# A Mamba-2 scan feeding a branch-train-merge FFN: the opening stage of the kernel in another order

## The chip, the cores and the metric

The kernel runs on one core of one Trainium2 chip. A core has five engines that run side by side, each with its own queue of instructions in order: TensorE (matrix products, called PE in the profile, with PEld for its weight loads), VectorE (DVE), ScalarE (ACT), GpSimd (POOL) and SyncE (SP), which here only issues DMA transfers. Engines wait for one another through semaphores. Products go to PSUM[...]; everything else works in SBUF, and the inputs, the outputs and some intermediate results lie in DRAM.

The metric is the device time of one execution in microseconds, as the median of several runs. "Chunk" is used below for 128 tokens of one sequence. "Step" is used for one half of one expert applied to one block of 512 tokens.

## The reference, cut to what matters

The first part is a Mamba-2 scan in chunks, the second a sum over four experts weighted by normalised probabilities.

```python
# x (4, 8, 768, 32), a (4, 8, 768), B and C (4, 8, 768, 16); all float32
log_a = np.log(np.clip(a, 1e-6, 1.0))
for each chunk:
    cum = np.cumsum(la, axis=-1)
    L = np.exp(cum[..., :, None] - cum[..., None, :]) * causal
    y_intra = einsum('bhij,bhjd->bhid', (C @ B^T) * L, x)
    y_inter = einsum('bhin,bhnd->bhid', C, state) * exp(cum)[..., None]
    y = y_intra + y_inter
    state = exp(sum(la)) * state + sum_j B_j x_j exp(cum[-1] - cum_j)

x = y.transpose(0, 2, 1, 3).reshape(3072, 256)        # heads side by side
p = probs / (probs.sum(-1, keepdims=True) + 1e-9)     # (3072, 4)
for e in range(4):                                    # w1 (4, 256, 1024), w2 (4, 1024, 256)
    out += p[:, e:e+1] * (maximum(x @ w1[e], 0) @ w2[e])
```

## The kernel before, in words

**Tiling.** The 3072 tokens are 24 chunks of 128. The four sequences go side by side: chunks 0 to 3 are the first chunks of the four sequences, chunks 4 to 7 their second ones, and so on, so that four chunks make a block of 512 tokens (`CPB = 4`), and there are six blocks. An FFN step takes one expert and one half of its hidden width, so a block has eight steps and the whole program 48, numbered n.

**The scan of a chunk c.** `load_tokens` (L104) brings x, B, B transposed and C transposed into `xb`. The decays a come to all 128 partitions in one of three ways, chosen by `spread` (L289) and `load_decays` (L109):

- for chunks 0 and 1 (below `SPREAD = 2`) a small tile `a_q` holds the rows, and TensorE spreads them over the partitions by a product with ones or with a mask, into the PSUM banks X and Y (chunk 0: also acc2 and acc3);
- for chunk 2 (below `DIRECT = 3`) a DMA reads the input a with a broadcast over the partitions into `ab` (512 KB written), and VectorE clips it and writes zeros in the first columns (L330, L331);
- from chunk 3 on a DMA reads the clipped copy `acut_d` in DRAM, which `store_decays` (L248) has written.

From the decays, `decay_part` (L315) makes the triangular decay matrices `LT` with two or four VectorE scans (L342), and GpSimd makes the weighted B columns of `MT` (L347). `masks` (L351, ScalarE) prepares C for two heads at a time, `scores` (L358, TensorE) makes C B^T in four PSUM banks, `masked` (L371, VectorE) multiplies scores and decays into `MT`, `outputs` (L379) multiplies `MT` by x on TensorE, and ScalarE copies the result into `yT`, the input of the FFN, and into `A`, from which `carry` (L405, VectorE) makes the state for the next chunk of the sequence.

**The FFN.** Its first products go to the banks X and Y and its second ones to the accumulators acc0 to acc3 (one PSUM bank each). Two PSUM banks with the tag `att` serve scores and outputs. Steps 0 and 1 (`PLAIN = 2`) are plain: `plain_first(n, b)` (L487) makes the first products of step n on half b of the block (256 tokens, two chunks), `gated` (L462, VectorE) does the maximum with zero and multiplies by the gate, and `plain_second` (L505) makes the second products. From step 2 on each step is a Strassen-like scheme with seven products instead of eight: `fmul`, `snap`, `total`, `diff`, `smul` (L434 to L517). It needs sums and differences of the block of inputs (`sums`, L421, four VectorE instructions) and of the weights. The latter are made on GpSimd in the first block (`sums_of`, L158) and stored to DRAM together with the weights, for the five blocks that follow.

**Gates.** The normalised probabilities are made by GpSimd, turned by TensorE and copied to `p_sb` (L264 to L266), and stored to DRAM as `p_d` by a DMA on ScalarE's queue (L267). `load_gate` (L281) reads a row from there with a broadcast to all partitions, on SP's queue. The gate of the first expert for the first block is made differently, by `spread_gate` (L269): four small products straight from `p_sb` and one ScalarE copy.

**What sets the order.** The schedule is written out by hand: each engine takes its instructions in the order in which the program's lines issue them. Lines 652 to 730 are the opening (four chunks, the two plain steps, and the first part of chunk 4). The loop at L733 then runs steps 2 to 47, with the pieces of later chunks between the products. Loads are issued on SP's queue in program order and may wait for a buffer[...].

Of the kernel before, what the change touches and what calls it, by code (L numbers as in the profile page):

```python
# [12 lines left out]
P = 128  # L13
NQ, NT = 4, 2
# [3 lines left out]
def kernel(  # L18
# [57 lines left out]
    def real(c):  # L76

        return c % CPB * NBLK + c // CPB
# [20 lines left out]


    st = {}
    SPREAD, DIRECT = 2, 3

    def load_tokens(c):  # L104
        xb = load.tile([P, W], FP32, tag="xb", name="xb", bufs=4)
        nc.sync.dma_start(out=xb, in_=xbc[real(c)])
        st.setdefault(c, {})["xb"] = xb

    def load_decays(c, queue):  # L109
        if c >= SPREAD:  # L110
            ab = load.tile([P, NH * P], FP32, tag="ab", name="ab")
            nc.sync.dma_start(
                out=ab, in_=(a if c < DIRECT else acut_d)[real(c)].rearrange(
                    "h s -> (h s)").partition_broadcast(P))
            st.setdefault(c, {})["ab"] = ab
        if c >= CPB:
            ah = st[c]["ah"] = load.tile([HN, P], FP32, tag="ah", name="ah")
            queue.dma_start(out=ah, in_=ac_d[real(c)].unsqueeze(1).to_broadcast([NH, N, P]))
# [61 lines left out]
    pr = const.tile([P, T // P, E], FP32, name="pr")  # L180
    a_sb = const.tile([NCH * NH // 2, 2, P], FP32, name="a_sb")

    a_q = const.tile([P, SPREAD, NT, P], FP32, name="a_q")
    nc.gpsimd.memset(a_q[:, 0], 0.0)
    nc.vector.memset(a_q[:, 1:], 0.0)
    nc.scalar.dma_start(out=pr, in_=probs)
# [5 lines left out]
        out=a_sb, in_=a.rearrange("c h s -> (c h) s").rearrange("(p r) s -> p r s", r=2))  # L192
    load_tokens(0)
    load_tokens(1)
    load_decays(2, nc.sync)
    load_w1(0)
    load_tokens(2)


    ident = const.tile([P, NQ, P], FP32, name="ident")  # L200
# [25 lines left out]
    def clip(engine, v, top=1.0):  # L226
        engine.tensor_scalar(out=v, in0=v, scalar1=1e-6, scalar2=top, op0=ALU.max, op1=ALU.min)
# [18 lines left out]
    nc.gpsimd.memset(a_cut[:, :, 0:1], 0.0)  # L246

    def store_decays():  # L248
        nc.sync.dma_start(
            out=acut_d.rearrange("c h s -> (c h) s").rearrange("(p r) s -> p r s", r=2), in_=a_cut)  # L250
        nc.sync.dma_start(
            out=ac_d.rearrange("c h s -> (c h) s").rearrange("(p r) s -> p r s", r=2), in_=a_sb)

    gate = {}
# [5 lines left out]
    def turn_gates():  # L260

        rows = T // P * E
        pp = ps_att.tile([rows, P], FP32, tag="att", name="pp")
        nc.tensor.transpose(pp, pr.rearrange("p i e -> p (i e)"), ident[:, 0])  # L264
        gate["rows"] = p_sb = const.tile([rows, P], FP32, name="p_sb")
        nc.scalar.copy(out=p_sb, in_=pp)  # L266
        nc.scalar.dma_start(out=p_d.rearrange("i e s -> (i e) s"), in_=p_sb)  # L267

    def spread_gate():  # L269

        p_sb = gate["rows"]
        g = ps_att.tile([P, CPB, P], FP32, tag="att", name="gp")
        for i in range(CPB):
            r = real(i) * E
            nc.tensor.matmul(
                out=g[:, i], lhsT=ident[:T // P * E, 0, r:r + 1].to_broadcast([T // P * E, P]),
                rhs=p_sb, start=(i == 0), stop=True, skip_group_check=True)
        gate[0, 0] = ffn.tile([P, CPB, P], FP32, tag="gate", name="gate", bufs=3)
        nc.scalar.copy(out=gate[0, 0], in_=g)
# [6 lines left out]

    yT, yS = {}, {}

    def spread(c):  # L289


        s = st[c]
        if c == 0:
            s["a"] = []
            for q, (pool, tag) in enumerate(((ps_f, "X"), (ps_f, "Y"), (ps_s, "acc2"), (ps_s, "acc3"))):
                k = slice(32 * q, 32 * q + 32)
                b = pool.tile([P, NT * P], FP32, tag=tag, name="a")
                nc.tensor.matmul(
                    out=b, lhsT=ones[k], rhs=a_q[k, c].rearrange("p t s -> p (t s)"),
                    start=True, stop=True, tile_position=(32 * q, 0))  # L300
                s["a"].append(b)
            return
        b = [ps_f.tile([P, 2, NT * P], FP32, tag=tag, name="a") for tag in ("X", "Y")]
        for q in range(NQ):
            nc.tensor.matmul(
                out=b[q // 2][:, q % 2], lhsT=qmask[:, q, 0:1].to_broadcast([P, P]),
                rhs=a_q[:, c].rearrange("p t s -> p (t s)"), start=(q % 2 == 0), stop=True,
                skip_group_check=True)
        s["a"] = [v.rearrange("p q s -> p (q s)") for v in b]

    def decays(c):
        for part in range(3):
# [2 lines left out]
    def decay_part(c, part):  # L315
# [10 lines left out]
            return  # L326
        half = NH * P // 2
        if part == 0:
            if SPREAD <= c < DIRECT:
                clip(nc.vector, s["ab"])  # L330
                nc.vector.memset(s["ab"].rearrange("p (h s) -> p h s", h=NH)[:, :, 0:1], 0.0)  # L331
            if c >= SPREAD:
                s["a"] = [s["ab"][:, :half], s["ab"][:, half:]]
            LT = att.tile([P, NH * P], FP32, tag="LT", name="LT", bufs=1)
            s["LT"] = LT.rearrange("p (h s) -> p h s", h=NH)

            s["MT"] = att.tile([P, NH, P + N], FP32, tag="MT", name="MT")
# [149 lines left out]
    def plain_first(n, b, a=(0, 1)):  # L487

        k = n // SPB
        cols = slice(b * HB - HB, b * HB)  # L490
        f = first.setdefault(n, {})
        for bank, ws in [(("X", (A11, A12)), ("Y", (S3, A22)))[i] for i in a]:
            f[bank] = ps_f.tile([P, JJ, HB], FP32, tag=bank, name=bank)
            for j in range(JJ):
                for i, w in enumerate(ws):
                    nc.tensor.matmul(  # L496
                        out=f[bank][:, j], lhsT=wt1[n][:, w, j * P:j * P + P],
                        rhs=yT[k][:, i, cols], start=(i == 0 and j == 0), stop=(i == 1),
                        skip_group_check=True)
# [157 lines left out]
    scores(0, homes)  # L657
    decays(0)
    spread(1)
    load_tokens(3)  # L660
    store_decays()
    load_w1(1)
    load_w2(0)
    load_decays(3, nc.sync)
    masked(0, range(NQ))
    divide_gates()
    sum_w1(0, 0)
    masks(1)
    decays(1)
    turn_gates()  # L670
    scores(1, banks)
    spread_gate()
    outputs(0, ps_att, "att")
    load_w2(1)
    load_w1(2)
    load_w2(2)
    sum_w1(1, 0)
    masked(1, range(NQ))
    outputs(1, ps_att, "att")
    masks(2)  # L680
    load_chunk(4)
    load_gate(0, 1)
    load_w1(3)
    load_w2(3)

    plain_first(0, 1, (0,))
    scores(2, banks)
    plain_first(0, 1, (1,))
    decays(2)
    sum_w2(0, 0)  # L690
    masked(2, range(NQ))
    masks(3)
    outputs(2, ps_att, "att")
    load_chunk(5)
    gated(0, "11", "X")

    scores(3, homes)
    decays(3)
    sum_w2(1, 0)
    gated(0, "21", "Y")  # L700
    plain_first(1, 1)
    masked(3, range(NQ))
    plain_gated(1, 1)
    plain_second(0, 1, 1)
    outputs(3, ps_att, "att")
    sum_w1(2)
    sum_w2(2)
    load_w1(4)
    load_w2(4)
    plain_second(0, 1, 2)  # L710
    masks(4)
    plain_first(0, 2)
# [12 lines left out]
    scores(4, ((ps_att, "att"), (ps_att, "att"), (ps_f, "X"), (ps_f, "Y")))  # L725
    masked(4, (2, 3, 0, 1))
    plain_second(1, 1, 2)
    sums(0)
    for c in range(1, CPB):
        carry(c)  # L730


    for n in range(PLAIN, NS):  # L733
# [127 lines left out]
```

## Time and profile before

| what | value |
|---|---|
| median of 5 runs | 667.01 us (665.47 to 667.9) |
| the profiled execution | 667.01 us, of which the span on the page is 665.2 us |
| TensorE busy | 648.1 us, 97% of the span, 3359 products |
| VectorE busy | 497.5 us, 75% |
| ScalarE and GpSimd busy | 115.7 us and 115.3 us, 17% each |
| DMA | 127.34 MB, mean 191 GB/s |

The page's chain follows the work that ended last back to the start, and says what share of the span each engine holds in it. In the listings by time, each row is a merged group of instructions of one line: its start and length in microseconds, the engine, the line of the kernel, what it writes and reads, how many, and in brackets how long the engine sat idle before it and what released it. A TensorE product in 32-bit numbers shows as two records, so four products of a bank show as x8. "Granted clock" is the share of TensorE's full clock in a stretch.

### The profile page before, as it was taken

To read this page: it belongs to the slowest core of one execution; us is meant where nothing else is said; L and a number is where in the kernel's file an instruction comes from. 1 tells how busy PE (TensorE), PEld (TensorE's weight loads), DVE (VectorE), ACT (ScalarE), POOL (GpSimd) and SP (SyncE) were. 2 spreads that over 40 slices of the span, in tenths; PEclk is the share of its full clock that TensorE was granted. 3 is DMA by queue.
4 is the path that set the end of the run, shared out by engine and by line. 5 is a ranking of instruction groups with operands and counts; after the bars stand their busy time and mean duration, and the time that the engine had idled before them with its cause. 6 is when DMAs were issued, how large, how long until landed. Compare 5 with 4: busy or idle time off the path is not lost.

```text
span 665.2 us, 8906 instructions
## 1 busy us (share of the span) xinstructions
PE 648.1 (97%) x3359; PEld 542.4 (82%) x3359; DVE 497.5 (75%) x813; ACT 115.7 (17%) x247; POOL 115.3 (17%) x157
## 2 busy tenths in 40 slices
PE   7999999999999999999999999999999999999997
PEld 4777878888888887888887888888788888888886
DVE  7488798787787688867878778678867776856655
ACT  3111211122112121221121112212111112111110
POOL 5776494020000002000003000000200000200000
PEclk9898999999999999999999999999999999999999
DMA  8987999414768610678640556941266862077000
GB/s 254 317 325 293 354 361 310 153 46 130 241 221 329 225 56 17 241 248 293 246 160 1 191 181 232 361 182 56 76 238 192 299 212 76 17 243 240 6 1 32
DMA packets 68274, 127.34 MB, mean 191 GB/s; under 512 B 26616, under 2 KB 50056, under 8 KB 68232
## 3 DMA queue, kind: packets, MB, share of 16 engines
q1 hardware_dynamic: 65404, 111.77, 48.9%
q0 software_dynamic: 2304, 14.68, 5.3%
q8 instruction: 26, 0.43, 0.3%
q10 hardware_dynamic: 524, 0.34, 0.2%
q14 instruction: 16, 0.13, 0.1%
HBM read 108.69 MB, written 18.07 MB: 191 GB/s over the span
## 4 chain that ended last, share of the span: by engine, by line
PE 87%; DVE 9%; issue 1%; DMA 1%; POOL 1%; ACT 0%; SPq 0%; ACTq 0%; DVEq 0%; POOLq 0%
PE acc L532 39%; PE X L448 22%; PE Y L448 18%; DVE hT L477 3%; PE g L365 2%; PE y L394 2%; DVE MT L375 1%; PE acc L513 1%; PE X L496 1%; PE Y L496 1%; DVE z L460 1%; PE y L388 1%; DVE h L470 1%; DMA wt<-in_w_dram 1%; DMA a_sb<-in_a_dram 0%
## 5 line engine op out<-in xcount | busy, mean ns | idle before, releaser
L532 PE MATMUL acc<-hT,wt 128*128 128x256 f32 x736 | 183.1, 382 | 0.0
L460 DVE TENSOR_TENSOR z<-Y,snap 128x512 f32<-128x512 f32 x138 | 94.5, 685 | 116.3 <-ACT snap L455 99.1
L455 ACT COPY snap<-X 128x512 f32<-128x512 f32 x138 | 80.9, 586 | 476.6 <-PE X L448 476.6
L532 PEld LDWEIGHTS acc<-hT,wt 128*128 128x128 f32 x736 | 138.3, 190 | 24.0 <-issue 6.0
L448 PE MATMUL X<-yS,wt 128*128 128x256 f32 x552 | 142.4, 381 | 0.0
L532 PE MATMUL acc<-h,wt 128*128 128x256 f32 x552 | 141.5, 379 | 0.0
L448 PEld LDWEIGHTS X<-yS,wt 128*128 128x128 f32 x552 | 105.5, 191 | 14.5
L532 PEld LDWEIGHTS acc<-h,wt 128*128 128x128 f32 x552 | 104.9, 190 | 14.3
L470 DVE SCALAR_TENSOR_TENSOR h<-z,gate 128x512 f32<-128x512 f32 x138 | 98.8, 716 | 3.5 <-PE acc L513 0.4
L448 PE MATMUL Y<-yT,wt 128*128 128x256 f32 x368 | 94.4, 379 | 0.0
L477 DVE TENSOR_TENSOR hT<-h,hT 128x512 f32<-128x512 f32 x92 | 76.3, 829 | 3.2
L448 PEld LDWEIGHTS Y<-yT,wt 128*128 128x128 f32 x368 | 68.8, 190 | 10.6
L477 DVE TENSOR_TENSOR hT<-h,h 128x512 f32<-128x512 f32 x92 | 63.5, 714 | 0.8
L448 PE MATMUL Y<-yS,wt 128*128 128x256 f32 x184 | 50.8, 399 | 8.9 <-DVE z L460 8.9
L342 DVE TENSOR_TENSOR_SCAN LT<-ab,ident 128x512 f32<-128x512 f32 x44 | 54.9, 1250 | 0.2 <-POOL MT L347 0.2
L347 POOL TENSOR_TENSOR MT<-xb,LT 128x128 f32<-128x128 f32 x20 | 8.7, 434 | 251.9 <-PE Y L448 133.8
L375 DVE TENSOR_TENSOR MT<-g,LT 128x256 f32<-128x256 f32 x96 | 33.9, 415 | 20.8 <-PE g L365 20.8
L448 PEld LDWEIGHTS Y<-yS,wt 128*128 128x128 f32 x184 | 33.4, 192 | 19.2 <-DVE z L460 12.7
L448 PE MATMUL X<-yT,wt 128*128 128x256 f32 x184 | 47.3, 380 | 0.0
L325 POOL TENSOR_TENSOR cts<-ctm,dec 128x256 f32<-128x256 f32 x20 | 18.5, 926 | 161.5 <-ACT snap L455 158.2
L470 DVE SCALAR_TENSOR_TENSOR h<-X,gate 128x512 f32<-128x512 f32 x50 | 34.3, 686 | 10.0 <-PE X L496 5.3
L448 PEld LDWEIGHTS X<-yT,wt 128*128 128x128 f32 x184 | 34.9, 190 | 5.1 <-DVE MT L375 0.3
(96 smaller groups left out, 341.8 us busy)
## 6 DMA issues: line engine op xcount, KB each, us to landing
wt<-w_d SPq DMA_DIRECT2D x80, 896.0 KB, 10.3
w_d<-wt POOLq DMA_DIRECT2D x16, 896.0 KB, 7.1
ab<-acut_d SPq DMA_DIRECT2D x21, 512.0 KB, 5.3
wt<-in_w_dram SPq DMA_DIRECT2D x32, 256.0 KB, 7.1
xb<-in_xbc_dram SPq DMA_DIRECT2D x24, 320.0 KB, 4.7
gate<-p_d SPq DMA_DIRECT2D x23, 256.0 KB, 9.5
out_dram<-ot SPq DMA_DIRECT2D x160, 16.0 KB, 5.3
ah<-ac_d SPq DMA_DIRECT2D x20, 64.0 KB
```

What stands on the lines that cost most here:

```text
L325: nc.gpsimd.tensor_mul(cts, s["ctm"], dec.unsqueeze(1).to_broadcast([HN, NT, P]))
L342: nc.vector.tensor_tensor_scan(out=LT[:, i * w:i * w + w], data0=s["a"][i], data1=ident.rearrange("p h s -> p (h s)")[:, :w], initial=0.0, ...
L365: nc.tensor.matmul(out=g.rearrange("p t s -> p (t s)"), lhsT=s["xb"][k, OBT:OBT + P], rhs=s["ctm"][k].rearrange("p t s -> p (t s)"), start ...
L375: nc.vector.tensor_mul(s["MT"][:, h, 0:P], s["g"][q], s["LT"][:, h])
L394: nc.tensor.matmul(out=y[32 * q:32 * q + 32, t, 0:w], lhsT=xb[:, h * D:h * D + D], rhs=MT[:, NT * q + t, 0:w], start=(first and t == 0), s ...
L448: nc.tensor.matmul(out=f[bank][:, j], lhsT=wt1[n][:, w, j * P:j * P + P], rhs=rhs, start=(i in (1, 2, 5) and j == 0), stop=(j == JJ - 1), ...
L455: nc.scalar.copy(out=s, in_=first[n]["X"])
L460: nc.vector.tensor_add(z, first[n]["Y"], first[n][i])
L470: nc.vector.scalar_tensor_tensor(out=h, in0=first[n][src], scalar=0.0, in1=g.unsqueeze(1).to_broadcast([P, JJ, HB]), op0=ALU.max, op1=ALU. ...
L477: nc.vector.tensor_sub(h[o], h[x], h[y])
L496: nc.tensor.matmul(out=f[bank][:, j], lhsT=wt1[n][:, w, j * P:j * P + P], rhs=yT[k][:, i, cols], start=(i == 0 and j == 0), stop=(i == 1), ...
L532: nc.tensor.matmul(out=acc[k, u][:, half], lhsT=w2_op(n, w)[:, j], rhs=rhs[:, j], start=(begins and j == 0), stop=(n % SPB == SPB - 1 and ...
```

## The change

Five things change, all in the opening stage and in what follows from it:

- **Third chunk's decays.** `SPREAD` goes from 2 to 3 and `DIRECT` is gone: chunk 2 takes its decays through `a_q` and TensorE, as chunk 1 does, in two halves (bank X, bank Y) that can be issued apart. The broadcast load of a for chunk 2 and VectorE's clip of it are gone. `a_q` has room for three chunks and lies in the buffer that the tile `o` uses later.
- **Loads.** On SP's queue the four `xb` loads of chunks 0 to 3 and the weights of steps 0 and 1 (`w1`) and of step 0 (`w2`) are issued at the start, with chunks 0 to 2 ahead of the first weights. The stores of `store_decays` move from SP's queue to ScalarE's.
- **Banks.** The first products of step 0 on half 1 go to acc2 and acc3 instead of X and Y.
- **Gates.** `spread_gate` is gone; the first gate is fetched from `p_d` by `load_gate(0, 0)` on SP's queue.
- **Order.** GpSimd's first weight sums come after the decays of chunk 2, the scores of chunk 2 come before the first FFN products, the gated products of step 0 come after the decays of chunk 3, `sums(0)` comes before the second half of the plain stage instead of after it, and of the carries of chunks 1 to 3 only the first stays there; those of chunks 2 and 3 go to the ends of steps 3 and 4.

```diff
-    SPREAD, DIRECT = 2, 3
+    SPREAD = 3
@@ load_decays
-                out=ab, in_=(a if c < DIRECT else acut_d)[real(c)].rearrange(
+                out=ab, in_=acut_d[real(c)].rearrange(
@@
-    a_q = const.tile([P, SPREAD, NT, P], FP32, name="a_q")
+    a_q = ffn.tile([P, SPREAD, NT, P], FP32, tag="o", name="a_q", bufs=1)
@@
     load_tokens(0)
     load_tokens(1)
-    load_decays(2, nc.sync)
+    load_tokens(2)
     load_w1(0)
-    load_tokens(2)
+    load_tokens(3)
+    load_w1(1)
+    load_w2(0)
@@ store_decays
-        nc.sync.dma_start(
+        nc.scalar.dma_start(
...
-        nc.sync.dma_start(
+        nc.scalar.dma_start(
@@
-    def spread_gate():
...
-    def spread(c):
+    def spread(c, halves=(0, 1)):
...
-        b = [ps_f.tile([P, 2, NT * P], FP32, tag=tag, name="a") for tag in ("X", "Y")]
-        for q in range(NQ):
-            nc.tensor.matmul(
-                out=b[q // 2][:, q % 2], lhsT=qmask[:, q, 0:1].to_broadcast([P, P]),
...
+        for i in halves:
+            b = ps_f.tile([P, 2, NT * P], FP32, tag="XY"[i], name="a")
+            for q in range(2):
+                nc.tensor.matmul(
+                    out=b[:, q], lhsT=qmask[:, 2 * i + q, 0:1].to_broadcast([P, P]),
...
@@ decay_part
-            if SPREAD <= c < DIRECT:
-                clip(nc.vector, s["ab"])
-                nc.vector.memset(s["ab"].rearrange("p (h s) -> p h s", h=NH)[:, :, 0:1], 0.0)
@@ plain_first
-            f[bank] = ps_f.tile([P, JJ, HB], FP32, tag=bank, name=bank)
+            pool, tag = (ps_f, bank) if n or b > 1 else (ps_s, {"X": "acc2", "Y": "acc3"}[bank])
+            f[bank] = pool.tile([P, JJ, HB], FP32, tag=tag, name=bank)
@@ the opening
     spread(1)
-    load_tokens(3)
-    store_decays()
-    load_w1(1)
-    load_w2(0)
-    load_decays(3, nc.sync)
     masked(0, range(NQ))
     divide_gates()
-    sum_w1(0, 0)
     masks(1)
+    store_decays()
     decays(1)
     turn_gates()
     scores(1, banks)
-    spread_gate()
+    masks(2)
+    spread(2, (0,))
     outputs(0, ps_att, "att")
+    spread(2, (1,))
+    sum_w1(0, 0)
+    masked(1, range(NQ))
+    outputs(1, ps_att, "att")
+    load_decays(3, nc.sync)
     load_w2(1)
     load_w1(2)
     load_w2(2)
+    scores(2, homes)
+    plain_first(0, 1)
+    decays(2)
     sum_w1(1, 0)
-    masked(1, range(NQ))
-    outputs(1, ps_att, "att")
-    masks(2)
+    masks(3)
+    load_gate(0, 0)
     load_chunk(4)
     load_gate(0, 1)
     load_w1(3)
     load_w2(3)
-    plain_first(0, 1, (0,))
-    scores(2, banks)
-    plain_first(0, 1, (1,))
-    decays(2)
-    sum_w2(0, 0)
     masked(2, range(NQ))
-    masks(3)
     outputs(2, ps_att, "att")
-    load_chunk(5)
-    gated(0, "11", "X")
     scores(3, homes)
     decays(3)
-    sum_w2(1, 0)
-    gated(0, "21", "Y")
+    load_chunk(5)
+    load_w1(4)
+    load_w2(4)
+    sum_w2(0, 0)
+    plain_gated(0, 1)
     plain_first(1, 1)
     masked(3, range(NQ))
+    sum_w2(1, 0)
     plain_gated(1, 1)
+    outputs(3, ps_att, "att")
     plain_second(0, 1, 1)
-    outputs(3, ps_att, "att")
     sum_w1(2)
     sum_w2(2)
-    load_w1(4)
-    load_w2(4)
+    sums(0)
     plain_second(0, 1, 2)
...
     plain_second(1, 1, 2)
-    sums(0)
-    for c in range(1, CPB):
-        carry(c)
+    carry(1)
@@ the loop over steps
+        if PLAIN < n <= CPB:
+            carry(n - 1)
         if c_out is not None:
             carry(c_out)
```

More of the change, by code (lines that the diff above doesn't have):

```diff
@@ L264, in turn_gates @@
         nc.tensor.transpose(pp, pr.rearrange("p i e -> p (i e)"), ident[:, 0])
-        gate["rows"] = p_sb = const.tile([rows, P], FP32, name="p_sb")
+        p_sb = const.tile([rows, P], FP32, name="p_sb")
         nc.scalar.copy(out=p_sb, in_=pp)
         nc.scalar.dma_start(out=p_d.rearrange("i e s -> (i e) s"), in_=p_sb)
-    def spread_gate():
[L271 to L274, printed above, removed]
-            nc.tensor.matmul(
[L276 to L279, printed above, removed]
     def load_gate(k, e):
@@ L302, in spread @@
             return
-        b = [ps_f.tile([P, 2, NT * P], FP32, tag=tag, name="a") for tag in ("X", "Y")]
-        for q in range(NQ):
-            nc.tensor.matmul(
-                out=b[q // 2][:, q % 2], lhsT=qmask[:, q, 0:1].to_broadcast([P, P]),
-                rhs=a_q[:, c].rearrange("p t s -> p (t s)"), start=(q % 2 == 0), stop=True,
-                skip_group_check=True)
-        s["a"] = [v.rearrange("p q s -> p (q s)") for v in b]
+        for i in halves:
[3 more added lines that the diff above has]
+                    out=b[:, q], lhsT=qmask[:, 2 * i + q, 0:1].to_broadcast([P, P]),
+                    rhs=a_q[:, c].rearrange("p t s -> p (t s)"), start=(q == 0), stop=True,
+                    skip_group_check=True)
+            s.setdefault("a", []).append(b.rearrange("p q s -> p (q s)"))
     def decays(c):
```

## The prediction

> **What bounds the kernel now.** I read the page's chain first, then TensorE by time, then what its gaps wait for on VectorE and ScalarE, then the clock by stretches, then the DMA landings. The chain:
>
> ```profile
> PE 87%; DVE 9%; issue 1%; DMA 1%; POOL 1%; ACT 0%; SPq 0%; ACTq 0%; DVEq 0%; POOLq 0%
> ```
>
> TensorE sets the end; only its holes can be won. From 70 us on, the holes are at most 1.5 us each, and the instruction lists of the two programs as built agree there but for two carries. So the case is the first 70 us. I write (n, b) for the first products of step n on block half b, and c in brackets for a chunk: y(3), masked(3). TensorE by time (start, length, idle before and releaser in brackets):
>
> ```profile
> 14.98 0.70 PE L394 MATMUL y<-MT,xb 128*32 128x144 f32 x16 [1.93 <-POOL MT L347]
> 16.16 3.44 PE L496 MATMUL X<-yT,wt 128*128 128x256 f32 x8 [0.48 <-ACT yT L400]
> 20.36 1.99 PE L496 MATMUL Y<-yT,wt 128*128 128x256 f32 x8
> ...
> 50.66 2.07 PE L448 MATMUL Y<-yS,wt 128*128 128x256 f32 x4 [1.89 <-DVE z L460]
> 52.52 1.81 PE L448 MATMUL X<-yS,wt 128*128 128x256 f32 x4
> 68.18 1.13 PE L448 MATMUL Y<-yS,wt 128*128 128x256 f32 x4 [0.72 <-DVE z L460]
> ```
>
> Twice a hole is followed by matmuls of double length: 3.44 us against 1.99 for the same shape at 20.36. The clock by stretches (busy and count of PE, PEld, DVE, ACT, POOL; granted clock; DMA):
>
> ```profile
> 13.14:16.55 3.41, 1.08 (x18) 0.80 (x19) 3.17 (x5) 1.76 (x7) 2.85 (x4) 1.00 0.94 260
> 16.55:19.97 3.42, 3.42 (x12) 2.33 (x14) 0.51 (x1) 0.81 (x3) 3.26 (x5) 0.50 1.01 316
> 47.27:50.69 3.42, 1.53 (x22) 0.85 (x20) 3.32 (x7) 1.05 (x3) 2.78 (x5) 1.00 0.78 317
> 50.69:54.10 3.41, 3.41 (x8) 2.78 (x9) 3.00 (x2) 0.00 (x0) 3.23 (x4) 0.50 1.03 418
> 149.68:153.09 3.41, 2.04 (x9) 1.82 (x10) 3.16 (x6) 0.47 (x3) 0.95 (x2) 1.00 0.00 0
> ```
>
> A stretch busy for 1.08 or 1.53 of 3.41 us is followed by one at half clock, about 1.7 us lost each; one busy for 2.04 is not. The second hole comes from VectorE, where the sums of the block and three carries stand ahead of z:
>
> ```profile
> 42.88 1.40 DVE L426 TENSOR_TENSOR yS<-yT 128x256 f32<-128x256 f32 x1
> 44.31 0.83 DVE L427 TENSOR_TENSOR yS<-yT,yS 128x256 f32<-128x256 f32 x1
> ...
> 49.93 0.68 DVE L460 TENSOR_TENSOR z<-Y,snap 128x512 f32<-128x512 f32 x1
> ```
>
> ScalarE by time shows the gates' store p_d holding the queue, although p_sb was ready at 10.99:
>
> ```profile
> 10.73 0.26 ACT L266 COPY p_sb<-pp 96x128 f32<-96x128 f32 x1 [3.01 <-PE pp L264]
> 13.93 0.33 ACTq L267 DMA_DIRECT2D p_d<-p_sb  x1
> 14.30 0.59 ACT L279 COPY gate<-gp 128x512 f32<-128x512 f32 x1 [3.30 <-DMA wt<-in_w_dram]
> ```
>
> And the transfers of p_d (the store and two fetches of gates, to 60 us):
>
> ```profile
> DMA to landing us min/median/max: 6.3/6.5/10.6
> ```
>
> [...] L426 takes 1.40 us here, 0.42 at 129.83 with GpSimd idle.
>
> **The change, part by part.**
>
> *Start.* The VectorE memset of a_q doubles to 128x512: 128x128 takes 0.17, 128x256 0.27, so 0.48, 0.2 us later for all that follows. The third chunk's two clips and memset (2 x 0.28 + 0.06) lie in VectorE's 0.87 us wait before the first scan; without that cover they cost 0.6. VectorE drops the clip and memset of ab (0.68 + 0.07), off the path. Four spreads of 128x256 (four warm such products: 1.73 us) replace gp's four of 128x128 (1.16), in the idle time at 13 to 15; exposed they would cost 0.6.
>
> *GpSimd.* MT of chunk 1 no longer stands behind the first weight sums (L160 to L162, 2.3 us), so the 1.93 us hole goes. What is late next is ScalarE. acut_d and ac_d move to its queue after the second mask (7.72); the list of the changed program makes ac_d wait for xb of chunk 2 (about 8.2) and p_d wait for ac_d's landing. ac_d took 5.3 us: 8.4 + 5.3 = 13.7. Behind p_d stand masks(2) (0.69), yT and A of chunk 0 (0.57) and of chunk 1 (0.56), so X of product (0,1) starts near 16.3, as before. Bounds: 15.4 if the stores overtake the loads (then y of chunk 1 and its copies bind), 17.2 if ac_d takes 6.3. I take 16.3. scores(2), 0.83 us between X and Y before, are now done in that wait. In the window 13.14 to 16.55 TensorE has half a spread and y(1) until 14.5 (1.36), scores (0.5) and the start of X (0.25): about 2.1 of 3.41, near the 2.04 that kept its clock. So no half clock.
>
> *SP's queue.* It loses ab of chunk 2 (512 KB) and the two stores (issue 0.34 and 0.54), so the weights move up: w1(0), landed at 10.98 before, by about 10; w1(1), 14.55 before, by about 13. Both are there before their products: nothing. ab(3) waits on SP for acut_d's landing, which moves from 12.86 to about 13.5, with six weight loads queued behind it; its scan comes after masked(2), near 17.5, and it had landed at 19.39, so VectorE may wait a microsecond for it. That lies under the wait for the gate below. a_q in the buffer of o costs nothing, since o is first written at step 8.
>
> *Other banks.* acc2 and acc3 for (0,1) leave X and Y to (1,1), which can run before the gates come: (0,1), y(2), scores(3) with its 0.6 us wait for A, and (1,1) end at 16.3 + 3.46 + 0.63 + 1.27 + 3.46 + 0.2 = 25.3.
>
> *Gates by DRAM.* gate(0,0) came from gp's copy at 14.9; now p_d is stored (13.7 + 6.3 = 20.0 at most) and fetched through SP behind w2(1), w1(2), w2(2). Bytes decide: before, 5.78 MB up to w2(2) had landed at 23.99. After, 5.52 MB up to the gate: 0.26 MB less at 360 GB/s is -0.7, start +0.2[...]. It lands at 23.8; from 22 (no loss) to 30.6 (20.0 + 10.6). On VectorE masked(3) is queued behind both products with this gate, and y(3) on TensorE behind masked(3): gated 1.34 + masked 1.40 + y 0.63 (0.3 overlapped) + two second products 3.65 gives 23.8 + 6.7 = 30.5 for the start of (0,2). It was 32.02: -1.5.
>
> *Plain stage.* sums(0), 4.0 us, move ahead of the gated product of (0,2), into idle time that VectorE had from 28.6 to 33.9; they run near 28 to 32, and X of (0,2) is ready at 32.2. Two carries leave as well. With scores(4) at 39.3, masked(4) (1.42), carry(1) (0.5 to 1.2) and the snap of X (near 43.3) before it, z of step 2 ends at about 44.0; TensorE needs it at 48.77 - 1.5 = 47.3. That gives -1.89 for the hole and -1.75 for its half clock (3.51 us for work of 1.73). With the sums still uncovered z would end at 48.0, a hole of 0.7.
>
> *Carries.* carry(2) after step 3 lies before a z ended at 79.07 for a matmul of 80.37: 1.3 of cover. carry(3) after step 4 stands before the z that TensorE waited 1.50 us for at 96.24: +0.5 (0.20 + 0.29), up to 1.6 with GpSimd beside it. I take 0.5.
>
> *Later loads.* The gate's issue (0.39) and its wait for p_d stand on SP ahead of xb(4) and ab(4), issued at 19.47 and 20.21 before; they come within a microsecond of that, and ab(4) is first scanned near 33. No later weight is late either: w1(6) is summed from 82.06 and used at 106.7. Cover of over 10 us: nothing.
>
> Sum: -1.5 - 1.89 - 1.75 + 0.5 = -4.6 against the profiled execution's 667.01 (span 665.2 and 1.8 around it), which is also the median of the runs: 662.4.
>
> **Rivals.**
>
> *Half clock stays.* The new waits, near 15 and between 25 and 26.3, meet one window with too little work: +1.7, 664.1. For it: [...] 2.1 is close to 2.04. Against: each wait is shorter than 1.89.
>
> *The gate decides.* Slower from a landing at 28.4 (23.8 + 4.6). If p_d and its fetch take the longest rows, 14.0 + 6.3 + 10.6 = 30.9, (0,2) starts at 37.6, +5.6 - 3.1: 669.5. Against: 10.6 was met behind a full queue and weight stores at 31.6.
>
> *Given back.* VectorE stays behind at the ends of steps 2 to 4 (holes 0.72, 1.50, 0.36), since GpSimd's weight sums slow it and their pace is the loads', which don't move. TensorE then waits until the time at which it used to arrive, and nothing is left: 667.0. Against: 68.18's chain starts with a TensorE product (scores at 59.45) and moves along.
>
> *Better.* The gate at 22.2 and the 0.72 hole gone: -1.6 - 0.7 more, 660.1 to 661.
>
> **How the numbers follow.** Forecast 0.50 (its own range 661.2 to 663.6), half clock 0.20, better 0.12, given back 0.09, gate decides 0.09. The time is the first case's. Low 660.0 takes in "better", high 666.5 half clock and a gate two microseconds later; about 2 in 10 is outside. A difference under 0.2% (1.3 us) can't be told from none: faster 0.82, same 0.09, slower 0.09.
>
> **What would show it.** Right: one half-clock stretch fewer after 16 us and none near 50; VectorE's L470 of (0,1) waiting for the gate's DMA until 23 to 25; y(3) on TensorE held by masked(3); no hole at step 2; the hole after step 4 at 2 us. ScalarE's p_d at about 13.7 shows the wait for ac_d, at 11.5 the overtaking. Wrong: a gate after 28, a half-clock stretch in the new waits, or holes of steps 3 to 5 grown by more than 2 us together.

## The result and the profile after

The changed kernel takes 665.0 us in the median (663.37 to 668.27, 43 runs), the kernel before 666.15 us beside it (80 runs): a ratio of 0.9989, 95% interval 0.998 to 0.9999. The forecast was 662.4 us, with a range from 660.0 to 666.5. The time lies inside that range, but the change is a gain of a tenth of a per cent, barely clear of none, where seven tenths were forecast.

The profiled execution of the changed kernel takes 664.69 us (span 662.9), 2.32 us less than that of before. Its page's chain, where TensorE still carries the end:

```profile
PE 88%; DVE 8%; DMA 2%; issue 1%; SPq 0%; ACT 0%; POOL 0%; ACTq 0%; DVEq 0%; POOLq 0%
```

TensorE by time in the changed kernel (start, length, then idle time before it and its releaser in brackets; L485 and L502 are the plain stage's first and second products, L436 the first products of later steps, L376 and L382 the outputs y):

```profile
16.10 1.99 PE L485 MATMUL X<-yT,wt 128*128 128x256 f32 x8
...
23.48 1.89 PE L485 MATMUL Y<-yT,wt 128*128 128x256 f32 x8
28.18 0.92 PE L382 MATMUL y<-MT,xb 128*32 128x144 f32 x16 [2.80 <-DVE MT L363]
...
32.58 1.89 PE L485 MATMUL X<-yT,wt 128*128 128x256 f32 x8
...
49.25 1.13 PE L436 MATMUL Y<-yS,wt 128*128 128x256 f32 x4
...
91.31 0.70 PE L376 MATMUL y<-cts,M 128*128 128x256 f32 x2 [0.59 <-POOL cts L316]
...
93.87 1.13 PE L436 MATMUL Y<-yS,wt 128*128 128x256 f32 x4 [1.24 <-DVE z L448]
```

Three of the forecast's marks are there: X of (0,1) starts at 16.10 and runs at full length, nothing waits at step 2 (49.25, no bracket), and no stretch before the tail runs at half clock (the granted clock is 1.00 from 16.55 to 655 us, and 0.999 in the mean of the execution). One wait is longer than forecast: TensorE stands for 2.80 us before y(3), where the forecast's own sum leaves some 1.2 us (from 25.3 to 23.8 + 1.34 + 1.40), and (0,2) starts at 32.58 and not at 30.5. Why, VectorE by time shows:

```profile
25.75 0.69 DVE L458 SCALAR_TENSOR_TENSOR h<-X,gate 128x512 f32<-128x512 f32 x1 [5.16 <-PE Y L485]
...
26.95 1.41 DVE L363 TENSOR_TENSOR MT<-g,LT 128x256 f32<-128x256 f32 x4
```

VectorE idles for 5.16 us. The bracket names Y of (0,1), but that product had ended at 19.8, so it was another of the instruction's waits: the gate. Its way begins on ScalarE, which by time shows the store (L269):

```profile
13.66 0.31 ACTq L269 DMA_DIRECT2D p_d<-p_sb  x1
14.02 0.69 ACT L344 ACTIVATE ctm<-xb,tmask 128x128 f32<-128x128 f32 x2 [3.05 <-DMA ac_d<-a_sb]
```

It goes on in SP's queue, by time, with the fetch (L273) behind the last of the weights:

```profile
15.63 1.27 SPq L146 DMA_DIRECT2D wt<-in_w_dram  x2
18.88 0.37 SPq L273 DMA_DIRECT2D gate<-p_d  x1
```

And the landings of the gates that are fetched in the first 60 us:

```profile
DMA to landing us min/median/max: 6.3/7.4/11.9
```

The store is issued at 13.66, as forecast, and has landed by 18.88, when SP is let go (it had issued nothing since 16.90); the shortest fetch, 6.3 us, is the first one, so the gate lands at 25.2. Working down from there: (0,2) is 0.56 us later than before, not 1.5 earlier; y of chunk 5, in step 3, starts at 63.57 against 66.24 (2.67 earlier, since the hole and the half clock of step 2 are gone); y of chunk 6, in step 5, at 91.31 against 93.52 (2.21 earlier); TensorE ends at 658.79 against 661.10 (2.31 earlier).

### The profile page after: what moved, and what is told of

It is laid out like the page before. It is cut to its first block, busy times and chain, and to the rows that moved or that the text cites. A ratio compares the mean times of both kernels' runs of the same rounds, so it can differ in the third digit from the quotient of the medians.

```text
span 662.9 us, 8905 instructions
## 1 busy us (share of the span) xinstructions
PE 645.5 (97%) x3359; PEld 540.5 (82%) x3359; DVE 496.3 (75%) x814; ACT 115.1 (17%) x246; POOL 113.1 (17%) x157
## 4 chain that ended last, share of the span: by engine, by line
PE 88%; DVE 8%; DMA 2%; issue 1%; SPq 0%; ACT 0%; POOL 0%; ACTq 0%; DVEq 0%; POOLq 0%
PE acc L521 39%; PE X L436 22%; PE Y L436 18%; DVE hT L465 4%; PE g L353 2%; PE acc L502 2%; PE y L382 2%; DVE MT L363 1%; PE X L485 1%; PE Y L485 1%; PE y L376 1%; DMA xb<-in_xbc_dram 1%; DMA ac_d<-a_sb 1%; DVE z L448 1%; DVE h L458 0%
## 5 line engine op out<-in xcount | busy, mean ns | idle before, releaser
L436 PE MATMUL X<-yS,wt 128*128 128x256 f32 x552 | 141.7, 379 | 0.0
L436 PEld LDWEIGHTS X<-yS,wt 128*128 128x128 f32 x552 | 104.9, 190 | 14.3
L436 PE MATMUL Y<-yT,wt 128*128 128x256 f32 x368 | 94.4, 379 | 0.0
L436 PEld LDWEIGHTS Y<-yT,wt 128*128 128x128 f32 x368 | 68.8, 190 | 10.6
L436 PE MATMUL Y<-yS,wt 128*128 128x256 f32 x184 | 49.8, 393 | 6.8 <-DVE z L448 6.8
L436 PE MATMUL X<-yT,wt 128*128 128x256 f32 x184 | 47.2, 379 | 0.0
L436 PEld LDWEIGHTS Y<-yS,wt 128*128 128x128 f32 x184 | 32.9, 189 | 16.8 <-DVE z L448 10.3
L436 PEld LDWEIGHTS X<-yT,wt 128*128 128x128 f32 x184 | 35.0, 190 | 4.8
```

The source lines that it names most:

```text
L436: nc.tensor.matmul(out=f[bank][:, j], lhsT=wt1[n][:, w, j * P:j * P + P], rhs=rhs, start=(i in (1, 2, 5) and j == 0), stop=(j == JJ - 1), ...
```

## The experiments

Every kernel was timed in five rounds. The kernel before took 665.7 us (59 runs) beside the first four, 665.21 (25) beside the next four and 665.68 (35) beside the last four; ratios are to these.

| run | made from | median us | ratio, 95% interval |
|---|---|---|---|
| e1 | changed kernel, first gate by TensorE again | 663.75 | 0.9962 (0.9949 to 0.9974) |
| e2 | kernel before, sums early, two carries later | 665.55 | 0.9995 (0.9983 to 1.0008) |
| e3 | changed kernel, gate fetched first | 663.25 | 0.9954 (0.9933 to 0.9975) |
| e4 | e1, store of the gates later | 664.3 | 0.9966 (0.9952 to 0.9979) |
| e5 | changed kernel, cts ahead of the second weight sums | 663.86 | 0.9972 (0.9959 to 0.9985) |
| e6 | e1 and the same | 662.38 | 0.9949 (0.9933 to 0.9965) |
| e7 | e3 and the same | 661.15 | 0.9927 (0.9912 to 0.9943) |
| e8 | e2 and the same | 663.92 | 0.9973 (0.996 to 0.9985) |
| e9 | kernel before, hole of step 2 filled | 665.52 | 0.9997 (0.9982 to 1.0012) |
| e10 | kernel before, cts ahead of the second weight sums | 665.71 | 0.9998 (0.9981 to 1.0015) |
| e11 | e7, carries later | 659.16 | 0.9911 (0.9892 to 0.993) |
| e12 | kernel before, first gate by DRAM | 670.54 | 1.0085 (1.006 to 1.0109) |

The theory after comparing the two profiles: the gate's fetch cost the forecast its first term. The rival: the gate only hides that the gains are given back further on. The first four runs try both.

### e1: the first gate by TensorE again

```diff
+    def spread_gate():    # four products from p_sb into a bank att, one ScalarE copy: as before
...
     scores(1, banks)
+    spread_gate()
...
     masks(3)
-    load_gate(0, 0)
     load_chunk(4)
```

> The changed kernel with one part undone: the first gate comes from four TensorE products and a ScalarE copy again, not from DRAM. Theory (the wait for the first gate's DMA is what ate the gain): VectorE's gated product of (0,1) starts near 20.6 instead of 25.75, the 2.8 us hole before y(3) is gone, TensorE reaches (0,2) near 29.8 instead of 32.58, span 2.7 us shorter than the changed kernel's, and fewer runs with a half-clock stretch; median near 661.6. Rival (the hole only shows a lateness that the next wait takes over, in VectorE, GpSimd or the weights): (0,2) or step 2 is late all the same, and the time stays within 1 us of the changed kernel's 665.0.

Measured: 663.75 us, 0.9962. TensorE by time, around y(3) (here L394):

```profile
26.03 0.70 PE L394 MATMUL y<-MT,xb 128*32 128x144 f32 x16
...
30.21 1.89 PE L497 MATMUL X<-yT,wt 128*128 128x256 f32 x8
```

The hole before y(3) is gone and (0,2) starts at 30.21, 0.3 from the forecast's 30.5. TensorE ends at 656.73 instead of 658.79. So the late gate costs 2.06 us in the profile, just what the forecast missed in that term. The median gains less and misses the theory's 661.6 by 2 us. The granted clock says why in part: 16 of the 21 executions have a mean of 0.996 to 0.997, and the profiled one is among the five above. Executions with a like clock agree with the profile: at 0.999 or more 662.77 against the changed kernel's 664.44, at 0.996 to 0.997 664.09 against 666.36 (the two kernels were timed on different occasions).

### e2: the sums and carries of the change alone

```diff
     sum_w2(2)
     load_w1(4)
     load_w2(4)
+    sums(0)
     plain_second(0, 1, 2)
...
     plain_second(1, 1, 2)
-    sums(0)
-    for c in range(1, CPB):
-        carry(c)
+    carry(1)
...
+        if PLAIN < n <= CPB:
+            carry(n - 1)
         if c_out is not None:
             carry(c_out)
```

> The kernel before with one part of the change alone: the sums of the first block ahead of the second half of the plain stage, carries of chunks 2 and 3 at the ends of steps 3 and 4. Theory: the 1.89 us hole of step 2 goes, and with it the half-clock stretch that follows it in some runs; the hole after step 4 grows by up to 0.6. Time 1.5 to 3 us shorter than the kernel before, so this part alone gives more than the whole change's 1.2. Rival (VectorE is late at step 2 for another reason): less than 0.5 us.

Measured: 665.55 us, 0.9995: no gain, where the theory had 1.5 to 3 us. TensorE by time:

```profile
47.25 1.13 PE L448 MATMUL Y<-yS,wt 128*128 128x256 f32 x4
...
91.13 0.70 PE L388 MATMUL y<-cts,M 128*128 128x256 f32 x2 [2.09 <-POOL cts L325]
...
92.56 2.08 PE L448 MATMUL Y<-yS,wt 128*128 128x256 f32 x4
```

And GpSimd by time, the first of the weight sums and the cts that TensorE waits for:

```profile
79.70 0.80 POOL L160 TENSOR_TENSOR wt<-wt 128x256 f32<-128x256 f32 x1 [9.99 <-DMA wt<-in_w_dram]
...
90.36 0.71 POOL L325 TENSOR_TENSOR cts<-ctm,dec 128x256 f32<-128x256 f32 x1
```

The hole at step 2 is gone, as meant. But at step 5 TensorE now stands for 2.09 us before y of chunk 6, which it had reached without a wait before, and the products behind run at half clock (2.08 us for what takes 1.13; the mean granted clock of this execution is 0.997). It waits for cts, which GpSimd makes behind the weight sums of two steps (79.70 to 89.6), and these had waited 9.99 us for weights to land. TensorE came 4.4 us earlier than before (y of chunk 5 at 61.88 against 66.24), and cts only 2.1 (90.36 against 92.50): the loads had not moved as far.

### e3: the gate fetched ahead of the second weights

```diff
     load_decays(3, nc.sync)
+    load_gate(0, 0)
     load_w2(1)
...
     masks(3)
-    load_gate(0, 0)
```

> The changed kernel with the first gate's fetch issued on SP ahead of the weights w2(1), w1(2) and w2(2) instead of behind them. In the instruction list as built, the gates' store p_d then also waits for an earlier load than ac_d. Theory: the gate lands near 20 instead of 25.2, VectorE does not wait for it, TensorE reaches (0,2) near 29, span 3 to 3.5 us shorter than the changed kernel's. Rival (bytes: the weights pushed back by 3 us become the wait, at GpSimd's sums or at the second products): the time stays within 1 us of the changed kernel's.

Measured: 663.25 us, 0.9954; the span is 661.7 us, 1.2 shorter than the changed kernel's, where 3 to 3.5 were expected. (0,2) starts at 29.29, and TensorE has no wait for the gate any more. The fetch is issued at 14.32 instead of 18.88. Part of that was not aimed at: in the program as built ScalarE no longer waits for ac_d, and p_d goes out at 11.01. Step 5 takes back what it can: 2.36 us of waiting for cts before y of chunk 6, and half clock behind it (2.08 us for Y's 1.13).

### e4: the store of the gates behind the outputs of chunk 1

```diff
-        nc.scalar.dma_start(out=p_d.rearrange("i e s -> (i e) s"), in_=p_sb)
+    def store_gates():
+        nc.scalar.dma_start(out=p_d.rearrange("i e s -> (i e) s"), in_=gate["rows"])
...
     outputs(1, ps_att, "att")
+    store_gates()
```

> As the run with the first gate by TensorE, and the store of the gates p_d issued on ScalarE's queue after the copies of chunk 1, so that its wait holds back neither masks(2) nor those copies. Theory: ScalarE is not what binds there, since TensorE is busy from 10.4 to near 15.5 with the extra products; X of (0,1) starts within 0.5 us of the first run's and the time is equal to it within 0.7 us. Rival (ScalarE's wait for ac_d sets the start): 1 to 1.5 us shorter.

Measured: 664.3 us, 0.9966, not to be told from e1. ScalarE's wait for ac_d is gone, but yT of chunk 1 then waits 1.23 us for its product, and X of (0,1) starts no earlier (17.47 against 16.83 in e1). That wait was covered. Here, too, step 5 has a hole, of 2.23 us.

### e5 to e8: cts ahead of the second weight sums

The new theory: y of chunk 6 waits for GpSimd, whose order puts cts behind weight sums that wait for loads; whoever makes TensorE earlier runs into it. The rival is VectorE's pace: then the wait only moves behind y, to the next product that needs bank Y. The same edit was put on the changed kernel, on e1, e3 and e2:

```diff
         sum_w1(n + 2)
-        if n > PLAIN:
+        if n > PLAIN and n != CPB:
             sum_w2(n + 1)
...
             decay_part(c_in, 2)
+        if n == CPB:
+            sum_w2(n + 1)
```

> The changed kernel, but in step 4 GpSimd forms the last columns of MT and the cts of chunk 6 before the sums of the second weights of step 5 instead of after them. GpSimd's theory (the ground that TensorE wins before 70 us runs into y of chunk 6, which waits for GpSimd, whose weight sums go at the pace of the loads): the hole of 0.59 us before the product with cts near 91 us vanishes, the step's other hole (1.24) may take some of it, because the sums now run beside VectorE's differences; median 0.3 to 1 us below the changed kernel. VectorE's theory (VectorE, slowed by the weight sums, sets the pace): the hole only moves behind the cts product into the one before Y, no change.

> The same move together with the first gate by TensorE. GpSimd's theory: no hole before the product with cts (0.66 us before the move), fewer half-clock stretches after it, median 662 to 663 against 663.75 without the move. VectorE's theory: 663.75, the hole before Y grows to 2 us or so.

> The same move together with the first gate fetched ahead of the second weights. GpSimd's theory: the hole of 2.36 us before the product with cts goes and with it the half-clock stretch behind it: 661 to 662 against 663.25. VectorE's theory: the same wait turns up before Y, 663.25.

> The kernel before with sums(0) early and two carries later, and the same move. Without the move the hole at step 2 was gone and one of 2.09 us with a half-clock stretch behind it stood before the product with cts, at no gain. GpSimd's theory: now the gain forecast for the hole at step 2 appears, median 662.5 to 664.2 against 665.55, a ratio to the kernel before near 0.996. VectorE's theory: 665.55 again.

Measured: 663.86, 662.38, 661.15 and 663.92 us; three lie in the theory's ranges, and e5 gained slightly more than its range. TensorE by time in e8, from y of chunk 6 on:

```profile
89.97 0.59 PE L388 MATMUL y<-cts,M 128*128 128x256 f32 x2
...
91.59 1.13 PE L448 MATMUL Y<-yS,wt 128*128 128x256 f32 x4 [0.39 <-DVE z L460]
...
105.53 1.13 PE L448 MATMUL Y<-yS,wt 128*128 128x256 f32 x4 [1.59 <-DVE z L460]
```

And GpSimd by time in e8:

```profile
86.03 0.42 POOL L347 TENSOR_TENSOR MT<-xb,LT 128x128 f32<-128x128 f32 x1
87.49 1.03 POOL L325 TENSOR_TENSOR cts<-ctm,dec 128x256 f32<-128x256 f32 x1 [1.04 <-DMA gate<-p_d]
```

cts is made at 87.49 instead of 90.36, ahead of the second group of sums, and y waits for nothing. The rival has its part: a wait for VectorE (z, 1.59 us) stands at step 6, where VectorE's work ahead of z takes longer than in e2 (the two instructions on hT just before it 2.74 us against 1.83). That GpSimd's sums slow it there is argued, not shown. The balance is taken from y of chunk 5 to y of chunk 7, two fixed points of TensorE, without and with the edit: changed kernel 56.13 and 55.59 us, e1 56.28 and 55.57, e2 57.76 and 55.59, e3 58.41 and 54.92. The edit is worth 2.2 and 3.5 us where a wait of over 2 us for cts, with half clock behind it, stood without it (e2, e3), and 0.5 to 0.7 where the wait was 0.6 us. How early TensorE comes does not decide this alone: it reaches y of chunk 5 at 61.34 in e1 and at 61.88 in e2. Part of what the medians gain is clock: in e1 16 of 21 executions have a mean granted clock of 0.996 to 0.997, in e6 one of six, and in e5 none of nine.

### e9: the hole of step 2 filled

```diff
             outputs(c_out, ps_att, "att")
+        if n == PLAIN:
+            t = ps_att.tile([P, 4, P], FP32, tag="att", name="t")
+            for _ in range(3):
+                nc.tensor.matmul(out=t, lhsT=ones, rhs=ones.unsqueeze(1).to_broadcast([P, 4, P]),
+                                 start=True, stop=True)
         fmul(n, 5)
```

> The kernel before with three idle TensorE products of 128x512 (about 1.3 us, result unused) behind y of chunk 4, in the hole of 1.89 us at step 2; the waits stay as they are. Theory [...]: the half-clock stretch near 50 us is gone and its mean clock is about 0.002 higher; since not every execution has it there, the median falls by 0.6 to 1.7 us. Rival (the slow products at 50 us come from something else, such as the full DMA): no change.

The theory comes from the profile of before, where the stretch with this hole has 1.53 us of TensorE work in 3.42 and one at a granted clock of 0.50 follows.

Measured: 665.52 us, 0.9997. TensorE by time:

```profile
48.41 2.84 PE L777 MATMUL t<-ones 128*128 128x512 f32 x6
51.09 1.03 PE L448 MATMUL Y<-yS,wt 128*128 128x256 f32 x4
```

The stretch of 3.42 us behind the filler (busy and count of PE, PEld, DVE, ACT, POOL; granted clock; share of the DMA; GB/s):

```profile
50.08:53.50 3.42, 3.42 (x15) 2.51 (x14) 3.32 (x3) 0.49 (x1) 3.24 (x4) 1.00 1.02 415
```

In the profile the half clock behind the hole is gone, with the waits of VectorE as they were, and the full DMA alone does not bring it on (share 1.02 at clock 1.00). One profile does not show that the filler did it, since e10 below has the same hole without a filler and without half clock. The mean granted clock over the executions rises as the theory says, from 0.9951 (35 executions) to 0.9969 (14). The time does not show it: my filler took twice what I had reckoned (2.7 us instead of 1.3), so it delayed Y by 0.7 us (z was there at 50.4), and what is left lies inside the interval. The size of the half clock alone is not settled by this run.

### e10: the same in the kernel before

The edit of e5 to e8, on the kernel before.

> The kernel before with only the move on GpSimd (MT's last columns and cts of chunk 6 ahead of the weight sums of step 5's second weights). Theory: TensorE reaches y of chunk 6 just when GpSimd is done, so the move alone takes no wait away; ratio 0.998 to 1.001. Rival (the move is worth its microsecond by itself, and the gains of the runs with it are its own): 664.2, ratio 0.998 or less.

Measured: 665.71 us, 0.9998: nothing by itself (from y of chunk 5 to y of chunk 7, 55.75 and 55.30 us). TensorE by time, at step 2:

```profile
50.36 1.13 PE L448 MATMUL Y<-yS,wt 128*128 128x256 f32 x4 [1.91 <-DVE z L460]
```

The hole is that of the kernel before, 1.91 us for 1.89, but Y runs at full length (1.13 us, not 2.07). With e2 (0.9995) and e8 (0.9973) this closes the square: sums and carries alone bring nothing, GpSimd's order alone brings nothing, both together bring 1.3 to 1.8 us.

### e11: the carries later

```diff
         gated(n, "11", "z11")
+        while late:
+            carry(late.pop(0))
...
         if PLAIN < n <= CPB:
-            carry(n - 1)
+            late.append(n - 1)
         if c_out is not None:
-            carry(c_out)
+            late.append(c_out)
```

> The changed kernel with the gate fetched ahead of the second weights, the move on GpSimd, and the carries of every step put behind the next step's first gated product instead of at the end of the step. If the carries stand before the sum that releases bank Y, the holes before Y (0.47 and 1.57 us near 88 and 102, 1.37 near 143, 1.0 each three times later) shrink by 0.5 to 0.9 us each: 658 to 659.5. If VectorE's differences alone set them: 661.

Measured: 659.16 us, 0.9911, the fastest of all. VectorE by time:

```profile
86.97 0.68 DVE L448 TENSOR_TENSOR z<-Y,snap 128x512 f32<-128x512 f32 x1
...
88.29 0.20 DVE L399 STREAM_TRANSPOSE S<-A 128x32 f32<-128x32 f32 x1
88.53 0.58 DVE L406 TENSOR_TENSOR M<-S,qmask 128x128 f32<-128x128 f32 x1
```

z no longer stands behind the carry (S and M), and the holes of 0.47 us near 88 and 1.57 near 102 are gone; one of 0.48 near 104 is new. The holes at the ends of the later blocks (1.37 near 143, then 1.0 each) did not shrink: the carry is not what sets them.

### e12: the first gate by DRAM, alone

```diff
     scores(1, banks)
-    spread_gate()
     outputs(0, ps_att, "att")
     load_w2(1)
     load_w1(2)
     load_w2(2)
+    load_gate(0, 0)
```

> The kernel before with one part of the change alone: the first gate isn't spread by TensorE but fetched from DRAM behind the second weights. Theory (the fetch lands near 25, two to three microseconds after the products need it, and nothing behind takes that up): (1,1) and all behind it come 2 to 3.5 us later, median 667 to 668.5. Rival (the fetch is hidden under other waits, or the hole at step 2 takes it up): 665.2 to 665.8.

Measured: 670.54 us, 1.0085, some five microseconds slower, two more than expected. VectorE's first instruction with the gate, by time:

```profile
26.81 0.69 DVE L470 SCALAR_TENSOR_TENSOR h<-X,gate 128x512 f32<-128x512 f32 x1 [5.33 <-DMA gate<-p_d]
```

And TensorE's product that waits for it:

```profile
27.55 3.78 PE L496 MATMUL X<-yT,wt 128*128 128x256 f32 x8 [3.68 <-DVE h L470]
```

The wait is 3.68 us on TensorE, and the product behind it is at half clock (3.78 us for 1.99; the mean granted clock of this execution is 0.987). In the changed kernel a gate nearly as late (VectorE starts with it at 25.75) costs 2.8 us of waiting and no half clock in the profile. Its order runs (1,1) and both scans of chunk 3 ahead of the gate, so those parts of the change seem to soften a cost which another part brings in; no run took them out one by one.

## Why the prediction was wrong

The forecast had 4.6 us of gain, and the medians show 1.15. Of the 3.5 us between them, 2.3 are in the profile after (664.69 against 662.4), 0.9 come in because the execution from which the forecast started was slower than the median of its kernel (667.01 against 666.15), and 0.3 because the profiled execution of the changed kernel was faster than its median.

**The step that failed: "It lands at 23.8".** The gate landed at 25.2 and VectorE began at 25.75. With that, "gives 23.8 + 6.7 = 30.5 for the start of (0,2)" became 32.58, and the term of -1.5 became +0.56: an error of 2.06 us, nearly all of the 2.3. The 6.7 us held from VectorE's start (25.75 + 6.83). What was wrong was "Bytes decide". They nearly did for the loads ahead of the gate: the last of these, of w2(2), was issued at 16.28 and landed 7.4 us later, at 23.7. But the gate was not close behind it. SP had to wait for the store and issued the fetch at 18.88, and from there it took 6.3 us, no longer than the weight loads before it (7.3 to 7.4). The forecast had both parts in its own text and did not add them: a store landed at 20.0 at most and 6.3 for the shortest landing make 26.3. The store was even faster than reckoned (5.2 us at most), which saved 1.1 of that. Two terms of the 23.8 are weaker than they look. The page of before shows 360 GB/s from 66 to 100 us (354 and 361), but 326 to 330 from 10 to 22 us, where these loads run; that would make the -0.7 a -0.8. And 0.3 us for the small pieces of the gate was the author's estimate, which no trace or run shows.

The fetch of 256 KB in 512-byte pieces has a second effect, on what is queued behind it. A stretch of the changed kernel while it goes on:

```profile
22.00:24.00 2.00, 2.00 (x11) 1.77 (x10) 0.00 (x0) 0.00 (x0) 1.92 (x3) 1.00 0.45 149
```

The same stretch of e1, which has no such fetch at that time:

```profile
22.00:24.00 2.00, 2.00 (x10) 1.49 (x10) 1.42 (x5) 0.00 (x0) 1.84 (x4) 1.00 1.04 331
```

The last two columns are the point: while the gate comes in, the DMA engines are busy for 0.45 of the time and move 149 GB/s, with a chunk's loads queued behind; without it they move 331. In e3, where the fetch is issued at 14.32, the same dip lies at 16 to 18 (0.40 and 114 GB/s). A rival is that the queue ran dry because SP had stood for 2 us ahead of the fetch. It can be a part. But in the kernel before SP stands as long (17.39 to 19.47) and the DMA stays full after it (0.99 and 343 GB/s from 22 to 24); the dip comes with the fetch of a gate, issued at 21.70 (0.64 and 187 from 24 to 26). Why the engines idle is open: no run here changed the size of the pieces.

**The steps that held.** ScalarE's wait for ac_d and p_d at 13.7 (13.66); X of (0,1) at 16.3 (16.10) at full clock; (1,1) ending at 25.3 (25.37); y(3) held by masked(3); no wait before y of chunk 1, since GpSimd's first weight sums come behind the decays of chunk 1 (and not of chunk 2, as the section on the change has it); the hole of step 2 and its half clock gone (from y of chunk 4 to y of chunk 5 the program is 3.23 us shorter; 3.64 had been taken off); the wait after step 4 at 2 us (1.83 against 1.50, so +0.33 for the +0.5; but 0.59 of it is a wait for GpSimd, which the forecast did not have there, and what the carry costs by itself is not shown). With the gate in time the rest of the sum stands in one execution: the profiled one of e1 has a span of 660.9 us, which with the 1.8 around it is 662.7, against a forecast of 662.4. The median of e1 is 663.75.

**The second error: the half clocks were taken as sure.** "-1.75 (its half clock)" and "which is also the median of the runs" treat one execution as typical. The mean granted clock of each execution says otherwise (119 executions of the kernel before beside the experiments; the 43 of the changed kernel left 44 records, two of them alike, and one lies between the rows):

| mean granted clock | before: executions, median us | after: executions, median us |
|---|---|---|
| 0.999 or more | 8, 663.62 | 24, 664.44 |
| 0.996 to 0.997 | 61, 665.11 | 16, 666.36 |
| below 0.996 | 50, 667.39 | 3, 668.07 |

A stretch of 3.41 us at half clock takes 0.0026 off the mean of a span of 665 us, so by this estimate the rows are about none, one, and two or more. The profiled execution of before (0.995) had two, and belongs to the last row; most have fewer. And row by row the changed kernel is not faster: its gain is that it has fewer such stretches. The two columns are from different occasions, on which the kernel before itself differed by 0.5 to 0.9 us, so the 0.7 to 1.3 us by which "after" stands higher are not safe. They agree with the profiles all the same: between 16 and 112 us TensorE's holes sum to 4.47 us before and 5.72 after. So the 2.3 us that the profile after gains are two stretches at half clock, about 1.7 us each, less longer waits.

The length of a hole alone does not tell whether half clock follows. Two stretches of the changed kernel, across the hole of 2.80 us, and one of e10, with the hole of 1.91 us, each as long as a stretch at half clock in the profile of before (3.41 us):

```profile
23.38:26.79 3.41, 1.99 (x10) 1.41 (x8) 1.04 (x2) 0.00 (x0) 3.17 (x6) 1.00 0.97 329
26.79:30.20 3.41, 2.02 (x21) 1.61 (x22) 3.38 (x9) 1.05 (x4) 3.00 (x5) 1.00 1.04 284
...
46.79:50.20 3.41, 1.66 (x21) 0.97 (x19) 3.34 (x6) 1.05 (x3) 2.77 (x5) 1.00 0.74 303
```

In the changed kernel each of the two stretches has some 2 us of work (1.99 and 2.02), and the granted clock is 1.00 in both and in the one behind them (30.21 to 33.62). In e10 the stretch with the hole has 1.66 us of work, and Y behind it runs at full length (1.13 us); in the kernel before nearly the same hole left 1.53, and a stretch at 0.50 followed. What decides between the two was not shown. That the executions in the rows of the table differ by stretches of this kind is an estimate from their mean clock, since only one execution of each kernel has a profile.

**The rivals.** *Given back* was named with the wrong engine for part of it. It has its place in step 5: a wait for GpSimd's cts takes back 0.6 to 2.4 us of whatever TensorE gains before (y of chunk 5 to y of chunk 6 takes 27.28 us before, 27.74 after, 27.88 in e1, 29.25 in e2, 29.91 in e3, and 27.00, 27.00, 27.00 and 26.27 in e5, e6, e8 and e7). "No later weight is late either: w1(6) is summed from 82.06 and used at 106.7. Cover of over 10 us" looked at the products that use the weights and not at what is queued behind the sums on GpSimd. In the changed kernel this costs 0.59 us. It is no more than 0.66 in e1's profile, where TensorE comes to y of chunk 5 2.2 us earlier, since cts came 2.1 us earlier too (88.46 against 90.54); in e4 it is 2.23. Why the loads let GpSimd keep pace in the one and not in the other is open. *The gate decides* was the right mechanism with the wrong point: a gate at 25.2, and not at 28.4, took nearly half of the 4.6 us. *Half clock stays* did not show in the profile, but is there in the table's second row, 16 of the 44 records; where those stretches lie is not known. That its 664.1 is nearer to the measured 665.0 than the forecast's 662.4 is luck, since its gate is at 23.8 too. *Better* did not come.

## What to carry to other kernels

A wait that is won back is worth what the next wait leaves of it: before pricing one, look along each in-order queue for what stands behind work that waits for loads, since such work may not move as far as TensorE does (2.1 us for 4.4 in e2; e10 and e8 show what its place in the queue is worth). A product with a late operand that comes through DRAM needs the whole way counted (store, landing, issue, fetch), each part by a measured landing and not by bytes alone. And before taking a profiled execution as typical, look at the granted clock of the other executions: more than a third of this forecast was a stretch that only some of them have.

## What the runs showed that I had not expected

- In 2 us of the broadcast fetch of one gate (256 KB in 512-byte pieces) the DMA engines are busy for 0.40 to 0.64 of the time and move 114 to 187 GB/s, with other loads queued behind it (the changed kernel, e3, the kernel before).
- Taking a wait away can cost nothing in one place and turn into clock in another: a hole of 2.1 to 2.4 us before y of chunk 6 was followed by products at half clock in e2 and e3 (2.08 us for 1.13), and in e4, with 2.23 us there, the profile's mean granted clock is 0.997 as in these two; with holes of 0.6 us there (the changed kernel, e1) it is 0.999 and 1.0. Of two holes of 1.9 us at step 2, one was followed by half clock (the kernel before, 2.07 us for Y) and one was not (e10, 1.13).
- Moving one DMA's issue on SP (e3) changed a wait on ScalarE: p_d went out at 11.01 instead of 13.66, without its wait for ac_d's landing.
- A kernel that beats both came out of it: gate fetched first, cts ahead of the second weight sums, carries behind the next step's first gated product: 659.16 us, 0.9911 of the kernel before (0.9892 to 0.993).
